# Attention and feed-forward: the second batch's visit with all remainder tiles first, its loads moved to another queue

## The chip, the cores and the metric

The kernel runs on one core of a Trainium2 chip. The metric is device time in microseconds (us) for one execution of the whole program, inputs and output in the chip's main memory (HBM). A core has five engines that run their own instruction streams and meet at semaphores: TensorE (PE, matrix products; its weight loads are listed as PEld), VectorE (DVE), ScalarE (ACT), GpSimd (POOL) and SyncE (SP). SP, ACT and POOL each issue DMA transfers; a queue issues in program order, so an issue that must wait holds up those behind it.

## The reference, cut to what matters

There are 8 batches, 12 heads, 448 tokens, 64 numbers per head. Queries and keys are normalised, scored, put through a softmax and multiplied with the values; the heads are put side by side, and two projections with a leaky ReLU between them follow.

```python
q_n = q / (norm(q, axis=-1) + 1e-06)            # q, k, v: (8, 12, 448, 64) float32
k_n = k / (norm(k, axis=-1) + 1e-06)
scores = q_n @ k_n.T / tau                      # tau = 0.1
attn = exp(scores - max) / (sum + 1e-09)
x = (attn @ v) as (8 * 448, 768)
h = x @ w_in                                    # w_in: (768, 2048)
out = maximum(0.01 * h, h) @ w_out              # w_out: (2048, 768), out: (3584, 768)
```

## The kernel before, in words

**Pairs.** Heads are taken two at a time. A pair is one batch's two neighbouring heads; there are 48, six for each batch, numbered in order, so batch 0 has pairs 0 to 5, batch 1 has 6 to 11, batch 2 has 12 to 17. Of 448 tokens, 384 are the main part (three tiles of 128) and 64 the remainder. The tile `raw_sb` has six slots for raw queries and keys; pair s uses slot s mod 6.

**What happens to a pair.** `load_qk(s)` issues four DMAs on SP (main queries, main keys, and two for the remainder rows). `load_pairs(eng, x, part, s, n)` does the same for several pairs at once, on a queue that is given. `squares(s)` squares queries and keys on GpSimd, two instructions (L182). `sums(s)` adds them up on DVE, two reduces (L193). `norm(s)` does the rest: `roots` on ACT (L200, L201: logarithm and exponential), `normalise` on DVE (L217, L218, and L222 twice, which writes the bf16 tile `qn`), and `transposes`, from pair 10 on a transposing DMA on SP (L254) into `qkT`. Then it issues loads for a later pair, and `hold`, a tiny GpSimd copy that reads `qn` and so makes GpSimd wait for it, before the squares of later pairs are queued.

**Batches and chunks.** Attention of one batch produces 448 columns of the transposed input `xT`. The projections go by chunks: chunk 0 and the other even ones have 384 tokens (three rows of 128), the odd ones 512 (four rows). In the main loop (L774 to L823) step b does three things. `visit(b)` is the second projection of chunk b (L459), and between its matmuls the scores of batch b + 1 (`key_tiles`, L280), each followed by ACT's exponential (L292). `attend_batch(b + 1)` makes the softmax sums and the products with the values of that batch (L307, L320), ACT's reciprocals (L339, L340) and DVE's scalings into `xT` (L361). `firsts(b + 1)` is the first projection of chunk b + 1 (L384), with ACT's leaky ReLU into `hT` (L391). In what follows "the second visit" is `visit(1)`: it has the second projection of chunk 1 and the scores of batch 2, that is pairs 12 to 17.

**Score tiles.** A pair has three main key tiles, each needing only its own `qkT`. The remainder keys of two pairs share one tile, so there are three remainder tiles for a batch; that of pairs 16 and 17 (written `(s0 + 5, 3)`) needs both pairs' `qkT`. From the third visit on all three stand ahead of the visit's matmuls. In the first two visits the third stands at the end (L738, L739).

**PSUM.** Eight banks are dealt by `banks`, which takes the ones given out longest ago. A visit's row of 128 tokens uses a pair of banks; at its end DVE copies both halves to SBUF (L471), in the last row of a visit ACT copies one half. The attention that follows uses the bank pairs again: `rem_products` (L307) writes sixteen products with the remainder values, eight into one pair of banks and then eight into another.

**What sets the order.** Nothing is planned by the machine: the schedule is manual, and each engine executes its instructions in the order in which the program writes them. Work for other engines is woven between PE's matmuls by tables: `norms` in the main loop names what is written after the n-th matmul step of row i of a visit, the tuples `wide`, `three`, `four` and `four_late` where a score tile is put, and `between` what is written ahead of the m-th of sixteen steps of the first projection.

**The beginning and the end.** The first pair is squared in pieces (L526 to L534), while PE runs 20 warm-up matmuls (`fill`, L505); then its `qn` is transposed by PE (L236), copied by ACT (L548) and scored. The last row of the last chunk has its second half of 384 columns computed in two parts (`second`, L410 to L429), each copied by DVE (L427) and stored in two DMAs on SP and ACT.

Of the kernel before, what the change touches and what calls it, by code (L numbers as in the profile page):

```python
# [16 lines left out]
def kernel(  # L17
# [10 lines left out]
    nc = tc.nc  # L28
# [341 lines left out]
    def chunk_cols(c):  # L370
        return (0, MAIN) if c % 2 == 0 else (MAIN, 512)
# [38 lines left out]
    def second(c, ts, half):  # L410
        last = c == B - 1 and ts == chunk_cols(c)[1] // 128 - 1
        if half == 0:
            osb[c, ts] = osp.tile([128, D_model], F32, name="osb")
        o = osb[c, ts]
        parts = 2 if last and half == 1 else 1
        for i in range(parts):
            n = HALF // parts
            lo = half * HALF + i * n
            po2 = banks(1)
            for m in range(MT):  # L420
                nc.tensor.matmul(  # L421
                    out=po2[:, :n],
                    lhsT=hT[c][:, m, ts * 128 : (ts + 1) * 128],
                    rhs=w_out_sb[:, m, lo : lo + n],
                    start=(m == 0), stop=(m == MT - 1),
                )
            nc.vector.tensor_copy(out=o[:, lo : lo + n], in_=po2[:, :n])  # L427
            if half == 1 or last:
                store(o, c, chunk_cols(c)[0] + ts * 128, lo if last else 0, lo + n, parts > 1)  # L429

    def store(o, c, x, lo, hi, apart=False):
        end, row = x + 128, 0
# [94 lines left out]
    nc.vector.tensor_tensor(sqs[0][1], k_h, k_h, op=ALU.mult)  # L527
    sums(0, (1,))
    nc.scalar.activation(sqs[0][0][:, :, 3], q_h[:, :, 3], func=AF.Square)
    for lo, hi in ((0, 3), (3, 4)):  # L530
        nc.vector.tensor_reduce(
            ss[0][:, 0:8].rearrange("p (h t) -> p h t", h=2)[:, :, lo:hi],
            sqs[0][0][:, :, lo:hi], axis=AX.X, op=ALU.add,
        )  # L534
    roots(0)
    nc.scalar.activation(sqs[1][1], k_h1, func=AF.Square)
    nc.scalar.activation(sqs[1][0], q_h1, func=AF.Square)
# [149 lines left out]

    def attend_batch(b):
        if b == 1:
            load_qk(14)  # L690
            load_qk(15)
            sums(12)
        attend_two(b * NQ)
        if b == 1:
            norm(12)
        attend(b * NQ + 2)


    def norm(s, transposed=True):
        if s >= NSLOT:  # L700
            return
        roots(s)
        normalise(s)
        if transposed:
            transposes(s)
        for x in (12, 13) if s == 11 else (s + 4,) if s > 11 else ():
            load_qk(x)
        ahead = {7: (), 8: (), 9: (10, 11), 10: (), 11: (12, 13)}.get(s, (s + 2,))
        if ahead:
            hold(qn[s][:, 6, 0, 0:1])  # L710
        for x in ahead:
            squares(x)

    def firsts(b, begun, between):

# [8 lines left out]
    def visit(b, order, norms, between):  # L724


        s0 = (b + 1) * NPAIR
        tiles = [(s0 + p, ki) for p in range(NPAIR) for ki in range(3)]
        key_tiles([(s0 + 1, 3), (s0 + 3, 3)] + [(s0 + 5, 3)] * (b > 1))
        for i, (pairs, after) in enumerate(zip(order, between)):  # L730
            last = i == len(order) - 1
            for n, _ in enumerate(groups(b, pairs, 4 if len(pairs) > 1 else 1, last), 1):
                for _ in range(after.get(n, 0)):
                    key_tiles([tiles.pop(0)])
                for fn in norms.get((i, n), ()):
                    fn()
        assert not tiles
        if b < 2:  # L738
            key_tiles([(s0 + 5, 3)])  # L739

    def at(*steps):
# [2 lines left out]
    wide = (at(8, 13, 18, 24, 29, 35, 40, 45, 50, 55, 60), at(4, 8, 12, 16, 16, 21, 26))  # L744
    three = (at(9, 16, 16, 21, 26, 31), at(5, 10, 16, 16, 21, 26, 31), at(5, 10, 16, 16, 20))
    four = (at(9, 16, 16, 24), at(4, 10, 16, 16, 24), at(4, 10, 16, 16, 24), at(5, 10, 16, 16))
    four_late = (at(5, 11, 16, 16, 24),) * 3 + (at(6, 16, 16),)

    deals["apart"] = False
    attend(NQ - 1, [lambda: first(0, 2, range(2, KT - 2)), lambda: first(0, 3, range(KT - 2))])  # L750
# [23 lines left out]
    for b in range(B):  # L774
# [6 lines left out]
        order = [[((ts, 0), (ts, 1))] for ts in range(tokens)]  # L781
        if b == 0:
            order = [order[0] + order[1], order[2]]
        norms = {(0, 18): [lambda: norm(11)]}
        if b:
            norms = {}
            for i in range(tokens - 1 + (b == 1)):
                norms[i, 4 if tokens > 3 else 12] = [lambda s=ready: norm(s)]
                ready += 1
                norms[i, 20] = [lambda s=ready: sums(s)]  # L790
        else:
            ready += 2
        visit(
            b, order, norms,
            wide if b == 0 else four_late if b == 1 else three if tokens == 3 else four,
        )
        attend_batch(b + 1)
        for j in range((b + 2) * NQ, (b + 3) * NQ):
            load_v(j)
        load_v_rem(b + 2)  # L800
        s = ready
        between = {0: [lambda s=s: norm(s)], 1: [lambda s=s: sums(s + 1)]}
        if b == 0:
            between = {
                0: [lambda: sums(13)], 1: [lambda: norm(13), lambda: sums(14)],
                4: [lambda: norm(14), lambda: sums(15)], 7: [lambda: norm(15)],
                9: [lambda: sums(16)], 11: [lambda: norm(16)], 14: [lambda: sums(17)],
            }
            ready += 5
        elif tokens == 3:  # L810
            between.update({
                4: [lambda s=s: norm(s + 1), lambda s=s: sums(s + 2)],
# [46 lines left out]
```

## Time and profile before

| what | us |
|---|---|
| median of 3 runs (406.75 to 407.87) | 406.77 |
| the profiled execution's own time | 406.75 |
| its span, first to last instruction | 404.94 |
| PE busy / ACT / DVE / POOL | 397.6 / 264.9 / 188.1 / 140.1 |
| first visit, from its first matmul of the second projection to its last score | 50.4 to 69.5 |
| attention of batch 1 | 69.9 to 76.4 |
| first projection of chunk 1 | 76.4 to 97.2 |
| second visit | 97.2 to 122.4 |

The busy time of an engine is summed over the span. A matmul's time includes its passage through the array, so matmuls that follow each other overlap in the list; their starts are what shows the pace. A line of a timeline gives start, duration, engine, source line, operation, output and input with shapes, how many instructions were merged, and in brackets the idle time before and what ended it. A line of the waits gives who waited for whom, the total, the number of times and the longest. In a table by windows, the busy time of an engine is followed by the granted clock, the share of DMA time and GB/s. "DMA to landing" is counted from the start of the issue to the last piece's arrival.

### The profile page before, as it was taken

How to read it: one execution, taken by the hardware profiler on the slowest of the kernel's cores; microseconds unless marked ns; L12 is line 12 of the kernel's file. 1: busy time of each engine (PE TensorE's matmuls, PEld its weight loads, DVE VectorE, ACT ScalarE, POOL GpSimd, SP SyncE). 2: the span in 40 equal slices, each digit the busy share in tenths (PEclk: the TensorE clock that was granted, in tenths of full speed). 3: DMA queues.
4: the chain of work that ended last, by engine and by line, in shares of the span. 5: the costliest groups of instructions: out<-in, count | busy, mean ns of one | idle time of the engine just before them, and what ended most of it. 6: DMA issues, size and time to landing. Idle time of an engine off the chain costs nothing.

```text
span 404.9 us, 10159 instructions
## 1 busy us (share of the span) xinstructions
PE 397.6 (98%) x4086; PEld 225.4 (56%) x4096; DVE 188.1 (46%) x403; ACT 264.9 (65%) x458; POOL 140.1 (35%) x213
## 2 busy tenths in 40 slices
PE   8899999999999999999999999999999999999996
PEld 3335655444555555544886555544687555544564
DVE  6987723684655624454552626256361721130021
ACT  4997799556875689655876569745786559844200
POOL 4995533464344513343142513155122500000000
PEclk9999999999999999999999999999999999999999
DMA  7999999797789827576396844685386821110033
GB/s 188 249 226 244 214 186 219 181 183 179 157 190 153 148 62 180 117 129 170 76 181 141 126 117 120 157 117 138 90 174 120 95 45 40 40 41 2 0 78 79
DMA packets 100735, 54.21 MB, mean 134 GB/s; under 512 B 69424, under 2 KB 95440, under 8 KB 100688
## 3 DMA queue, kind: packets, MB, share of 16 engines
q1 hardware_dynamic: 76400, 40.13, 42.7%
q0 software_dynamic: 23440, 12.92, 23.5%
q8 instruction: 32, 0.52, 0.6%
q10 hardware_dynamic: 848, 0.52, 0.5%
q14 instruction: 15, 0.12, 0.1%
HBM read 45.61 MB, written 11.01 MB: 140 GB/s over the span
## 4 chain that ended last, share of the span: by engine, by line
PE 96%; ACT 1%; DVE 1%; issue 0%
PE ps L384 36%; PE ps L459 31%; PE ps L320 11%; PE ps L280 8%; PE ps L421 5%; PE ps L505 2%; PE ps L307 1%; ACT pe L292 1%; PE ps L236 1%; DVE qkT L261 0%; DVE qn L222 0%; ACT qkT L548 0%; ACT rb L340 0%; DVE warm L488 0%; DVE ss L193 0%
## 5 line engine op out<-in xcount | busy, mean ns | idle before, releaser
L384 PE MATMUL ps<-xT,w_in_sb 128*128 128x384 bf16 (+1 forms) x760 | 147.4, 352 | 0.4
L459 PE MATMUL ps<-w_out_sb,hT 64*128 64x384 bf16 x1536 | 144.0, 323 | 0.0
L292 ACT ACTIVATE pe<-ps 128x896 bf16<-128x896 f32 x144 | 124.4, 917 | 16.7 <-PE ps L280 14.9
L384 PEld LDWEIGHTS <-w_in_sb 128*128 128x128 bf16 x768 | 74.1, 98 | 71.5 <-issue 3.7
L391 ACT ACTIVATE hT<-ps 128x384 bf16<-128x384 f32 (+1 forms) x128 | 67.3, 543 | 67.2 <-PE ps L384 66.7
L459 PEld LDWEIGHTS <-hT 64*128 64x128 bf16 x1536 | 84.4, 94 | 44.7 <-PE ps L459 4.2
L182 POOL TENSOR_TENSOR sq<-raw_sb 128x512 f32<-128x512 f32 x90 | 82.7, 940 | 13.4 <-DMA raw_sb<-in_k_dram 12.6
L222 DVE TENSOR_TENSOR qn<-raw_sb,r 128x512 bf16<-128x512 f32 x96 | 56.8, 634 | 1.7
L280 PE MATMUL ps<-qkT 64*128 64x448 bf16 (+1 forms) x384 | 54.8, 353 | 1.6 <-DVE qkT L261 0.8
L193 DVE TENSOR_REDUCE ss<-sq 128x6 f32<-128x384 f32 (+1 forms) x95 | 54.5, 610 | 2.6 <-POOL sq L182 2.3
L471 DVE COPY osb<-ps 128x384 f32<-128x384 f32 x41 | 21.2, 553 | 69.7 <-PE ps L459 38.8
L514 POOL CAST seen<-qn 128x1 f32<-128x1 bf16 x44 | 8.2, 187 | 123.8 <-DVE qn L222 123.6
L217 DVE TENSOR_SCALAR ss<-ss 128x14 f32<-128x14 f32 x48 | 10.0, 209 | 73.9 <-ACT ss L201 73.8
L361 DVE TENSOR_TENSOR xT<-ps,rb 128x448 bf16<-128x448 f32 x48 | 27.7, 619 | 24.3 <-ACT rb L340 24.1
L160 POOL DMA_DIRECT2D v_b<-in_v_dram x24 | 18.6, 777 | 39.9 <-PE ps L320 39.9
L320 PE MATMUL ps<-pe,v_b 128*32 128x448 bf16 x576 | 32.0, 353 | 0.0
L280 PEld LDWEIGHTS <-qkT 64*128 64x128 bf16 (+1 forms) x384 | 17.8, 97 | 17.9 <-issue 6.6
L339 ACT ACTIVATE rb<-ps 128x448 f32<-128x448 f32 x24 | 12.9, 538 | 15.3 <-PE ps L320 14.3
L320 PEld LDWEIGHTS <-v_b 128*32 128x32 bf16 x576 | 15.1, 97 | 12.0 <-issue 0.6
L427 DVE COPY osb<-ps 128x384 f32<-128x384 f32 (+1 forms) x9 | 4.6, 513 | 36.6 <-issue 22.6
L421 PE MATMUL ps<-w_out_sb,hT 128*128 128x384 bf16 (+1 forms) x144 | 21.0, 308 | 0.0
L292 ACT ACTIVATE pr<-ps 128x896 bf16<-128x896 f32 x24 | 20.7, 923 | 0.2 <-PE ps L280 0.2
(52 smaller groups left out, 188.1 us busy)
## 6 DMA issues: line engine op xcount, KB each, us to landing
raw_sb<-in_q_dram SPq DMA_DIRECT2D x46, 192.0 KB, 3.3
raw_sb<-in_k_dram SPq DMA_DIRECT2D x44, 192.0 KB, 3.5
out_dram<-osb SPq DMA_DIRECT2D x30, 192.0 KB, 3.1
v_b<-in_v_dram POOLq DMA_DIRECT2D x24, 192.0 KB, 4.8
out_dram<-osb SPq DMA_DIRECT2D x12, 384.0 KB, 2.7
w_out_sb<-in_moe_w_out_dram POOLq DMA_DIRECT2D x4, 768.0 KB, 16.3
w_in_sb<-in_moe_w_in_dram POOLq DMA_DIRECT2D x3, 512.0 KB, 8.5
w_in_sb<-in_moe_w_in_dram POOLq DMA_DIRECT2D x2, 768.0 KB, 13.1
```

The lines of the kernel that those rows point to most:

```text
L182: eng.tensor_tensor(sq, x, x, op=ALU.mult)
L193: nc.vector.tensor_reduce(o.rearrange("p (h t) -> p h t", h=2), sqs[s][i], axis=AX.X, op=ALU.add)
L222: scalings[s] = nc.vector.tensor_tensor(qn[s][:, lo:hi], x.rearrange("p h t d -> p t h d"), r[:, r0 : r0 + 2 * nt].rearrange("p (h t) -> p ...
L280: nc.tensor.matmul(out=out[:, a, :S], lhsT=x[rows, c0:c1], rhs=x[rows, 0:S], start=True, stop=True,)
L292: nc.scalar.activation(out=dst, in_=sc[:, :, :S], func=AF.Exp, scale=inv_tau)
L320: nc.tensor.matmul(out=x[32 * g : 32 * g + 32, :S], lhsT=weights(g, ki) if ki < 3 else rem(g), rhs=pe[s][:, ki, a, :] if ki < 3 else pr[j] ...
L361: scalings[j, e] = nc.vector.tensor_tensor(xT[m][:, 2 * jj + e, half * S : (half + 1) * S], pos.pop((j, e))[:, :S], rbs[j], op=ALU.mult,)
L384: nc.tensor.matmul(out=pm[:, :n], lhsT=w_in_sb[:, kt, m * 128 : (m + 1) * 128], rhs=xT[c // 2][:, kt, c0 : c0 + n], start=(kt == 0), stop= ...
L391: nc.scalar.activation(out=hT[c][:, m, :n], in_=pms.pop((c, m))[:, :n], func=AF.Prelu, alpha=0.01)
L421: nc.tensor.matmul(out=po2[:, :n], lhsT=hT[c][:, m, ts * 128 : (ts + 1) * 128], rhs=w_out_sb[:, m, lo : lo + n], start=(m == 0), stop=(m = ...
L459: done[p][i] = nc.tensor.matmul(out=pos2[p][:, i, :HALF], lhsT=hT[c][rows, m, ts * 128 : (ts + 1) * 128], rhs=w_out_sb[rows, m, half * HAL ...
L471: copy(out=osb[c, ts][:, half * HALF : (half + 1) * HALF], in_=po2[:, i, :HALF])
```

## The change

Four things are changed.

- At the beginning, the squares of the first pair's keys go from DVE to ACT, between ACT's squares of its main and of its remainder queries; DVE sums them behind the first reduce of the queries.
- The last half row's two parts are 256 and 128 columns wide instead of 192 and 192.
- The second visit has all three remainder tiles at its beginning and uses the table `four` of the later visits; `four_late` goes. So pairs 12 to 17 are all normalised before it: `sums(12)` is written after step 26 of the first visit's last row, `norm(12)` ahead of the attention of batch 1 and `sums(13)` in its middle, and pairs 13 to 17 follow in the first projection of chunk 1. The second visit normalises three pairs instead of four.
- Pairs 14 and 15 are no longer loaded by SP at the beginning of `attend_batch(1)` but by four DMAs on GpSimd's queue, behind the squares of pair 12 and ahead of those of pair 13; pairs 16 and 17 by four more behind the squares of pair 14. SP's loads of pairs 19, 20 and 21 all follow the normalising of pair 17. The values of batch 2 are loaded (on GpSimd's queue, seven DMAs) at step 8 of the first projection, behind the squares of pair 18, instead of ahead of it.

```diff
     def second(c, ts, half):
-        parts = 2 if last and half == 1 else 1
-        for i in range(parts):
-            n = HALF // parts
-            lo = half * HALF + i * n
+        widths = (HALF * 2 // 3, HALF // 3) if last and half == 1 else (HALF,)
+        for i, n in enumerate(widths):
+            lo = half * HALF + sum(widths[:i])
...
     nc.scalar.activation(sqs[0][0][:, :, 0:3], q_h[:, :, 0:3], func=AF.Square)
-    nc.vector.tensor_tensor(sqs[0][1], k_h, k_h, op=ALU.mult)
-    sums(0, (1,))
+    nc.scalar.activation(sqs[0][1], k_h, func=AF.Square)
     nc.scalar.activation(sqs[0][0][:, :, 3], q_h[:, :, 3], func=AF.Square)
     for lo, hi in ((0, 3), (3, 4)):
         nc.vector.tensor_reduce(
...
+        if lo == 0:
+            sums(0, (1,))
...
     def attend_batch(b):
         if b == 1:
-            load_qk(14)
-            load_qk(15)
-            sums(12)
+            norm(12)
         attend_two(b * NQ)
         if b == 1:
-            norm(12)
+            sums(13)
         attend(b * NQ + 2)
...
     def norm(s, transposed=True):
-        for x in (12, 13) if s == 11 else (s + 4,) if s > 11 else ():
+        for x in {11: (12, 13), 14: (18,), 17: (19, 20, 21)}.get(s, (s + 4,) if s > 17 else ()):
             load_qk(x)
...
-        for x in ahead:
+        for i, x in enumerate(ahead):
             squares(x)
+            if s in (11, 12) and i == 0:
+                for part in range(2):
+                    for y in (q, k):
+                        load_pairs(gp, y, part, 14 + 2 * (s - 11), 2)
...
     def visit(b, order, norms, between):
-        key_tiles([(s0 + 1, 3), (s0 + 3, 3)] + [(s0 + 5, 3)] * (b > 1))
+        key_tiles([(s0 + 1, 3), (s0 + 3, 3)] + [(s0 + 5, 3)] * (b > 0))
...
-        if b < 2:
+        if b == 0:
             key_tiles([(s0 + 5, 3)])
...
-    four_late = (at(5, 11, 16, 16, 24),) * 3 + (at(6, 16, 16),)
...
-        norms = {(0, 18): [lambda: norm(11)]}
+        norms = {(0, 18): [lambda: norm(11)], (1, 26): [lambda: sums(12)]}
         if b:
-            for i in range(tokens - 1 + (b == 1)):
+            for i in range(tokens - 1):
...
         attend_batch(b + 1)
-        for j in range((b + 2) * NQ, (b + 3) * NQ):
-            load_v(j)
-        load_v_rem(b + 2)
+        def values(b=b + 2):
+            for j in range(b * NQ, (b + 1) * NQ):
+                load_v(j)
+            load_v_rem(b)
+        if b:
+            values()
...
             between = {
-                0: [lambda: sums(13)], 1: [lambda: norm(13), lambda: sums(14)],
-                4: [lambda: norm(14), lambda: sums(15)], 7: [lambda: norm(15)],
-                9: [lambda: sums(16)], 11: [lambda: norm(16)], 14: [lambda: sums(17)],
+                0: [lambda: norm(13)], 1: [lambda: sums(14)],
+                2: [lambda: norm(14)], 3: [lambda: sums(15)],
+                4: [lambda: norm(15)], 5: [lambda: sums(16)],
+                7: [lambda: norm(16)], 8: [lambda: sums(17), values],
+                9: [lambda: norm(17)], 13: [lambda: sums(18)],
             }
-            ready += 5
+            ready += 6
```

More of the change, by code (lines that the diff above doesn't have):

```diff
@@ L428, in second @@
             if half == 1 or last:
-                store(o, c, chunk_cols(c)[0] + ts * 128, lo if last else 0, lo + n, parts > 1)
+                store(o, c, chunk_cols(c)[0] + ts * 128, lo if last else 0, lo + n, len(widths) > 1)
     def store(o, c, x, lo, hi, apart=False):
@@ L792 @@
             ready += 2
[L793 to L796, printed above, removed]
+        visit(b, order, norms, wide if b == 0 else three if tokens == 3 else four)
         attend_batch(b + 1)
-        for j in range((b + 2) * NQ, (b + 3) * NQ):
-            load_v(j)
-        load_v_rem(b + 2)
+        def values(b=b + 2):
[4 more added lines that the diff above has]
+            values()
         s = ready
```

## The prediction, made before the result was known

> **What bounds the kernel now.** I read the page's busy times first, then TensorE's waits, then the timelines of the stages that the change touches.
>
> ```profile
> PE 397.6 (98%) x4086; PEld 225.4 (56%) x4096; DVE 188.1 (46%) x403; ACT 264.9 (65%) x458; POOL 140.1 (35%) x213
> ```
>
> ```profile
> PE ps L505 <- DVE warm L488: 1.5, 1, 1.5
> PE ps L280 <- DVE qkT L261: 0.8, 2, 0.5
> PE ps L280 <- ACT pe L292: 0.5, 2, 0.3
> PE ps L280 <- ACT qkT L548: 0.2, 1, 0.2
> PE ps L236 <- DVE qn L222: 0.2, 1, 0.2
> ```
>
> PE is busy for 98% of the span, and its waits are 3.2 us in all, every one of them before 24 us. From there to 401 us matmuls stand end to end, so anything that keeps PE waiting there is paid in full at the end, and what the other engines save there is worth nothing. Gains can only come from the opening, from fewer switches in PE's own order, and from the last store.
>
> The sum is made against the profiled execution: 406.75 us, of which 404.94 is the span and 1.81 lies around it; the median of the three runs is 406.77, so the two may be exchanged. About 0.3% (1.22 us) is what a measurement of this kernel can tell from no change.
>
> **Part 1, the opening: the first keys' squares go from DVE to ACT.**
>
> ```profile
> 4.37 0.56 DVE L527 TENSOR_TENSOR sq<-raw_sb 128x384 f32<-128x384 f32 x1 [1.66 <-DMA raw_sb<-in_k_dram]
> 4.96 0.55 DVE L193 TENSOR_REDUCE ss<-sq 128x6 f32<-128x384 f32 x1
> 5.43 0.74 DVE L531 TENSOR_REDUCE ss<-sq 128x6 f32<-128x384 f32 x2
> ...
> 8.06 0.59 PE L505 MATMUL ps<-warm 128*128 128x512 bf16 x2
> ...
> 8.49 0.28 PE L236 MATMUL ps<-id,qn 128*128 128x128 bf16 x2
> ```
>
> On ACT the square costs 0.52 us (its twin, L526), and fits between that one's end at 4.53 and the wait for the remainder rows, which ends at 5.40. DVE loses 0.56 us. The last reduce then waits only for ACT's remainder square (5.40 + 0.31 = 5.71) and ends near 6.02 instead of 6.17: pair 0's keys are normalised 0.15 us earlier. But the first transposes start at 8.49 behind the warm-up matmuls, with nothing waited for: their queries were ready near 7.97, their keys at 8.44, and the keys' turn comes only at 8.72. Everything after hangs on ACT's copy of those transposes. So I take 0.00; the warm-up is the cover. Ends: -1.7 us, all the waits listed above after the first, and +0.3, if the remainder square comes late by most of the keys' square.
>
> **Part 2, the end of the first visit: sums of pair 12 in front of a PSUM copy.** DVE now does pair 12's two reduces before the last copy of the visit; it did them after.
>
> ```profile
> 67.76 1.82 POOL L182 TENSOR_TENSOR sq<-raw_sb 128x512 f32<-128x512 f32 x2 [10.26 <-DMA raw_sb<-in_k_dram]
> 69.71 0.56 DVE L471 COPY osb<-ps 128x384 f32<-128x384 f32 x1 [5.47 <-PE ps L459]
> 70.05 0.65 PE L307 MATMUL ps<-pr,v_rem 64*32 64x448 bf16 x16
> 70.19 1.14 DVE L193 TENSOR_REDUCE ss<-sq 128x8 f32<-128x512 f32 x2
> ```
>
> GpSimd's squares of pair 12 run from 67.76 (they waited for the load, whose issue is not moved) to 69.58. The second reduce can start at 69.61; two reduces in a row stand 0.47 us apart from what follows, so the copy starts near 70.08 instead of 69.71. PE's sixteen remainder products use two bank pairs; the second pair is the one that this copy and ACT's copy empty. In the trace its second matmul starts at 70.32, 0.05 after the copy's end, so the copy is already what PE waits for. It moves to 70.64 + 0.05 = 70.69: **+0.37 us** on PE, where nothing else can run. Behind that copy wait also the third store (unhurried) and the matmuls after. Ends: 0 (the load lands 0.37 earlier) and +1.1 (both reduces, if it lands a few tenths later).
>
> Pair 12's normalisation before the attention hides: ACT's two root operations (0.31 + 0.21) fit between its exponential, which ends at 71.02, and the logarithm that starts at 71.43 and is itself pushed to 71.80. DVE's four (0.17 + 0.24 + 1.16 and gaps, 1.6 us) end near 73.1, where the scalings, pushed by 0.37 too, begin: 0.06 late, without a reader in haste.
>
> **Part 3, loads and squares during the second first-projection.** PE reaches the second visit at 97.25 + 0.37 = 97.62, and its third remainder tile, with pair 17, near 98.05. Before, that tile stood at 122.06. So pair 17's transposing DMA must have landed by 98.05. The chain:
>
> - GpSimd's four load issues cost 0.81 + 0.76 + 0.64 + 0.63 = 2.84 us (the same four at 28.88 to 31.67). The first four run 69.5 to 72.4 and push the squares of pair 13 from 69.5 to 72.4, where they cost nothing: DVE reads them at 75.2. Pairs 14 and 15 then land, by the 3.5 us of a lone GpSimd load and some 1.7 us for each 384 KB more at 230 GB/s, near 76.5; squares of 14 to 78.3; the next four issues to 81.2; squares of 15 to 83.2; pairs 16 and 17 land near 85; squares of 16 to 86.9, of 17 to 88.7.
> - DVE and ACT go in turn: normalise a pair (1.6 us), sum the next (1.1), roots (0.6), 3.3 us in all. From scalings that end at 77.7: pair 13 at 79.3, 14 at 83.2 (it waits for ACT's second hT), 15 at 86.6, 16 at 89.9, 17 at 93.2. GpSimd is ahead at each step, by 0.2 to 0.5 us for pairs 15 and 16. The transposing DMA of 17 is issued at 93.3. On SP it is behind those of 15 and 16 and the load of 18, all issued by 91.5; the loads of 19 to 21 now follow it.
>
> ```profile
> 187.76 1.26 SPq L254 DMA_TRANSPOSE qkT<-qn  x1
> ...
> DMA to landing us min/median/max: 3.0/5.5/6.9
> ```
>
> The first line is its like in the fourth batch, issued 3.93 us ahead of the visit at 191.69 and landed after 2.9. The second gives the four landings between 80 and 98 us. The high ones, 6.5 to 6.9, are those beside the second batch's value loads. The change moves these value loads to GpSimd's queue behind the squares of pair 18, that is to 92 to 97 us, just beside pair 17. Landing: 96.2 with 2.9, 97.8 with 4.5 (the middle of the ends 2.9 and 6.9, since SP's own loads no longer stand ahead), 100.2 with 6.9. I take 97.8: in time, **0.00**, ends 0 and +2.2 us.
>
> By the Trainium skill, DMA: Bandwidth & Descriptors, Queues, rings and completion order, each DMA engine goes round-robin between the queues that have work, packet by packet. By that rule the transpose shares the engines with the values and its own transfer would at most about double, which the 6.9 of the trace exceeds.
>
> ACT's hT passes wait up to 1.8 us for the roots of pair 17, hidden by eight banks of 1.3 us each. Value loads are needed by 123: hidden. Pair 19's load, now behind pair 17's transpose on SP, is squared by 102; the next PSUM copies behind its sums on DVE are due at 104.8: hidden, 2 us to spare.
>
> The moved loads are now issued by GpSimd. By the Trainium skill, SBUF — State Buffer, SBUF: two separate sides, a GpSimd-issued DMA can starve while DVE holds the port they share, 620 ns becoming some 3100. The four issues at 28.88 to 31.67 took 0.63 to 0.81 us with DVE busy beside them, so the trace does not bear it out.
>
> **Part 4, PE's order in the second visit.** It becomes that of the later four-row visits.
>
> ```profile
> 97.25:122.37 25.12, 25.12 (x305) 1.00 0.74 168
> 191.69:216.74 25.05, 25.05 (x307) 1.00 0.67 144
> ```
>
> From the first score to the attention's first product the second visit takes 25.12 us, its twin in the fourth batch 25.05 (and the one in the sixth): **-0.07**. The remainder products after it take 0.71 us to the next group (122.37 to 123.08) against 0.69 (216.74 to 217.43), since one wait on a DVE copy goes: **-0.02**. Ends 0 and -0.3.
>
> **Part 5, the last part is 256 + 128 columns instead of 192 + 192.** Start to start a matmul took 162.5 ns for 384 columns and 82.5 for 192; that line gives 109 and 56 (transposes of 128 columns: 56). 16 x (109 + 56) is 2.64 us, as is 32 x 82.5. The final copy shrinks by 64 columns:
>
> ```profile
> 398.74 0.56 DVE L427 COPY osb<-ps 128x384 f32<-128x384 f32 x1 [2.03 <-PE ps L421]
> ...
> 401.32 0.36 DVE L427 COPY osb<-ps 128x192 f32<-128x192 f32 x1 [0.89 <-PE ps L421]
> ```
>
> 0.201 us less for 192 columns less, so **-0.07**. The part before is stored 0.43 later but its issue on both queues (0.57) is over by 401.55, before the last copy ends at 401.6. Ends -0.2 and +0.3.
>
> **Sum.** 0.00 + 0.37 + 0.00 - 0.09 - 0.07 = +0.21; 406.75 + 0.21 = 406.96, say 407.0.
>
> **Rivals.**
> - Pair 17 lands late (slower). Place: third remainder tile of the second visit, PE waiting. From 98.05 each us is paid; it passes the 0.3% bound when the landing is later than 99.06, which is a latency over 5.7 or a chain 1.2 us behind. For: 6.9 and 6.5 stand in the trace beside value loads, and GpSimd's lead is thin. Against: those had loads ahead in SP's queue. At 6.9: 406.96 + 2.2 = 409.2. Chance 0.19.
> - The copy is not delayed (the load of pair 12 lands earlier, or DVE has done both reduces): 406.96 - 0.37 = 406.6. Against: GpSimd's start at 67.76 is the load's landing. Chance 0.12.
> - GpSimd's eight load issues take longer beside DVE's work: a tenth more for each uses up the lead of 0.2 to 0.5 us, and 2 us beyond give 409. Against: the longest issue on GpSimd's row is 0.85 us. Chance 0.04. (It is what the page on SBUF would have.)
> - The opening does hang on the first keys' squares (faster): all 1.7 us of PE's waits go, 406.96 - 1.7 = 405.3; it decides from 1.4 on. Against: the warm-up in front. Chance 0.05.
>
> **Numbers.** The forecast has 0.60. Faster by over 0.3%: 0.05; slower: 0.19 + 0.04 = 0.23; within: 0.72. Low end 406.4: the second rival less 0.2 from the open ends. High end 408.7: about half of the slower cases. Left out: 0.05 below, some 0.12 above.
>
> **What would show it.** First transposes at 8.49 as before; the L471 copy near 70.1 and the second bank's remainder products near 70.7; the second visit 25.05 long; its third remainder tile with no wait on a DMA; a last copy of 0.29 us. Wrong if PE shows a wait of more than 1 us near 98, or if hT passes hold it between 80 and 97.

## The result, and the profile after

The changed kernel takes 416.66 us, the median of six runs (415.73 to 418.61), where the kernel before takes 406.83 beside it. The ratio is 1.024, 95% interval 1.022 to 1.027: it is slower by 2.4%, and the forecast of 407.0 and its range were wrong. The profiled execution of the changed kernel took 418.61 us with a span of 416.8. It is 2 us above the median of its runs, so the terms below add up to 11.9 us, the difference of the two profiled spans, and not to 9.8. Many lines of the code have moved up by one: L459 is now L458, L471 is L470, L427 is L426, L505 is L504.

The page's busy times and the granted clock, the lines of it that answer to the first fence of the prediction:

```profile
PE 402.2 (96%) x4096; PEld 226.4 (54%) x4096; DVE 192.6 (46%) x402; ACT 265.1 (64%) x459; POOL 146.9 (35%) x221
...
PEclk9999999999599999999999999999999999999999
```

PE has nearly the same list of matmuls and is busy 4.6 us longer, and in one slice its clock was granted at half. TensorE's waits in the changed kernel:

```profile
PE ps L280 <- DMA qkT<-qn: 6.7, 1, 6.7
PE ps L504 <- DVE warm L487: 1.5, 1, 1.5
PE ps L307 <- DVE osb L470: 1.1, 1, 1.1
PE ps L280 <- DVE qkT L261: 0.6, 2, 0.3
...
PE ps L458 <- DMA w_out_sb<-in_moe_w_out_dram: 0.2, 1, 0.2
```

Before, the list had the warm-up and tenths of a microsecond at the start. Two new lines stand out: 6.7 us for a transposing DMA at the scores, and 1.1 us for DVE's PSUM copy at the remainder products. TensorE by stages (stretch, length, busy time and matmuls, clock, DMA share, GB/s), the first projection of chunk 1, the second visit, and a part of that visit:

```profile
78.47:99.30 20.83, 20.83 (x101) 1.00 0.51 117
99.30:134.43 35.13, 28.34 (x305) 0.85 0.90 164
107.50:112.70 5.20, 5.20 (x36) 0.50 0.78 195
```

The first projection is as long as before (76.42 to 97.25 was 20.83 too). The second visit took 25.12 and now takes 35.13: 6.79 us idle, and 3.22 us more busy time for the same matmuls. The last line says why: at a clock of 0.50 each matmul takes twice as long. By finer stretches the clock fell at about 102.6, in the middle of the wait, and rose again at about 112.8. From the end of the wait at 107.04 on that is 5.8 us of work at half clock, and half of it, 2.9, is the loss. The account of the 11.9 us:

| where | us | read from |
|---|---|---|
| start of the first visit, 50.43 to 50.72 | +0.29 | differs from run to run (50.28 to 50.79 in the profiles below that keep `hold`) |
| rest of the first visit | +0.42 | 0.2 of it is the wait for a load of `w_out` |
| the copy ahead of the remainder products | +1.34 | the sixteen remainder products with the values at L307, 1.92 instead of 0.58 |
| first projection of chunk 1 | 0.00 | 20.83 in both |
| second visit, idle | +6.79 | 35.13 - 28.34 |
| second visit, longer matmuls | +3.22 | 28.34 - 25.12, of which 2.9 by the clock |
| all that follows | -0.16 | the remainder |

The copy first. The timeline of the changed kernel at the end of the first visit:

```profile
69.45 1.82 POOL L182 TENSOR_TENSOR sq<-raw_sb 128x512 f32<-128x512 f32 x2 [11.67 <-DMA raw_sb<-in_k_dram]
70.52 1.34 DVE L193 TENSOR_REDUCE ss<-sq 128x8 f32<-128x512 f32 x2 [5.58 <-POOL sq L182]
71.77 0.55 DVE L470 COPY osb<-ps 128x384 f32<-128x384 f32 x1
72.37 0.38 PE L307 MATMUL ps<-pr,v_rem 64*32 64x448 bf16 x7 [1.07 <-DVE osb L470]
```

The mechanism is as forecast: DVE waits 5.58 us for the squares, the PSUM copy stands behind the two reduces, PE behind the copy. But the load of pair 12 landed at 69.45 where I had taken 67.76 as fixed, and PE itself was 0.7 later.

Now pair 17. Instructions on the tile `qkT` between 98 and 108 us, with who waited and the time from issue to landing; then TensorE's timeline after the wait:

```profile
L254 SPq DMA_TRANSPOSE qkT<-qn x1: 1242/1242/1242, 99.2 to 99.2; - x1
...
  PE ps L280: 6.7, 1
...
DMA to landing us min/median/max: 7.8/7.8/7.8
```

```profile
107.04 0.58 PE L280 MATMUL ps<-qkT 64*64 64x448 bf16 x2 [6.72 <-DMA qkT<-qn]
107.55 3.06 PE L458 MATMUL ps<-w_out_sb,hT 64*128 64x384 bf16 x18
```

The transposing DMA is issued at 99.19 and lands at 106.99. PE begins the second visit at 99.30 and stands before the third remainder tile from 100.32 on. Two things made it late. The issue stands 20.7 us after the first projection's beginning (78.47) where the prediction had 16.5 (93.3 less 76.79). And the landing took 7.8 us where it had 4.5. Why the issue is late is in the timelines of GpSimd and DVE, and in DVE's waits between 78 and 100 us:

```profile
79.34 0.17 DVE L217 TENSOR_SCALAR ss<-ss 128x14 f32<-128x14 f32 x1
79.78 2.27 POOL L182 TENSOR_TENSOR sq<-raw_sb 128x512 f32<-128x512 f32 x2 [3.41 <-DMA raw_sb<-in_k_dram]
79.81 2.66 DVE L222 TENSOR_TENSOR qn<-raw_sb,r 128x512 bf16<-128x512 f32 x2
82.00 0.81 POOL L127 DMA_DIRECT2D raw_sb<-in_q_dram  x1
...
84.14 0.66 DVE L217 TENSOR_SCALAR ss<-ss 128x14 f32<-128x14 f32 x1 [0.62 <-ACT ss L201]
84.93 2.30 POOL L182 TENSOR_TENSOR sq<-raw_sb 128x512 f32<-128x512 f32 x2
85.11 2.53 DVE L222 TENSOR_TENSOR qn<-raw_sb,r 128x512 bf16<-128x512 f32 x2
...
89.03 1.04 POOL L182 TENSOR_TENSOR sq<-raw_sb 128x512 f32<-128x512 f32 x1 [1.14 <-DMA raw_sb<-in_k_dram]
...
97.14 0.52 DVE L217 TENSOR_SCALAR ss<-ss 128x14 f32<-128x14 f32 x1 [0.62 <-ACT ss L201]
97.57 2.31 POOL L160 DMA_DIRECT2D v_b<-in_v_dram  x3
```

```profile
DVE ss L217 <- ACT ss L201: 2.5, 4, 0.6
DVE xT L361 <- ACT rb L340: 0.2, 1, 0.2
```

GpSimd waits 3.41 us for pair 14, whose load, issued from 71.2 on, came at 79.7 instead of 76.5; 1.7 of these 3.2 us are the later start, since pair 12 had landed late. Only behind the squares of pair 14 can the loads of pairs 16 and 17 be issued (82.0), and they land at 88.9 instead of 85.

Yet DVE did not wait for any of these squares: its waits in this stretch are for ACT alone. What the late data did was to move GpSimd's squares and load issues beside DVE's normalising, and there DVE's rows grow. The two multiplies (L222) take 1.16 us together when no square runs beside them; here they took 2.66 for pair 13, beside the squares at 79.78, and 2.53 for pair 14, beside those at 84.93. The small L217, 0.17 alone, took 0.45 to 0.79 in pairs 14 to 17. Over the five pairs these rows took 11.54 us where alone they would take 6.65, 4.9 us more. With the scalings before them, which end at 79.4 instead of 77.7, that is why pair 17's normalising begins at 97.14 instead of 91.6 (93.2 less 1.6). The last line of the timelines is the values, issued from 97.57 on, right beside the transposing DMA.

The end answers to Part 5. DVE's last copies in the changed kernel:

```profile
412.54 0.42 DVE L426 COPY osb<-ps 128x256 f32<-128x256 f32 x1 [1.20 <-PE ps L420]
413.37 0.29 DVE L426 COPY osb<-ps 128x128 f32<-128x128 f32 x1 [0.40 <-PE ps L420]
```

### The profile page after: what moved, and what is told of

It reads as the page before. It is cut to its first block, busy times and chain, and to the rows that moved or that the text cites. A ratio compares the mean times of both kernels' runs of the same rounds, so it can differ in the third digit from the quotient of the medians.

```text
span 416.8 us, 10146 instructions
## 1 busy us (share of the span) xinstructions
PE 402.2 (96%) x4096; PEld 226.4 (54%) x4096; DVE 192.6 (46%) x402; ACT 265.1 (64%) x459; POOL 146.9 (35%) x221
## 4 chain that ended last, share of the span: by engine, by line
PE 81%; DMA 13%; POOL 3%; ACT 2%; issue 1%; DVE 1%; POOLq 0%
PE ps L384 31%; PE ps L458 28%; PE ps L320 10%; PE ps L280 6%; PE ps L420 5%; DMA w_out_sb<-in_moe_w_out_dram 4%; DMA w_in_sb<-in_moe_w_in_dram 4%; DMA qkT<-qn 2%; DMA raw_sb<-in_q_dram 2%; POOL sq L182 1%; ACT pe L292 1%; PE ps L307 1%; DMA raw_sb<-in_k_dram 1%; POOL raw_sb L132 0%; POOL v_rem L167 0%
## 5 line engine op out<-in xcount | busy, mean ns | idle before, releaser
L458 PE MATMUL ps<-w_out_sb,hT 64*128 64x384 bf16 x1536 | 146.7, 327 | 0.2 <-DMA w_out_sb<-in_moe_w_out_dram 0.2
L458 PEld LDWEIGHTS <-hT 64*128 64x128 bf16 x1536 | 85.3, 95 | 46.4 <-issue 5.4
L391 ACT ACTIVATE hT<-ps 128x384 bf16<-128x384 f32 (+1 forms) x128 | 66.4, 544 | 62.2 <-PE ps L384 61.9
L182 POOL TENSOR_TENSOR sq<-raw_sb 128x512 f32<-128x512 f32 x90 | 83.8, 951 | 23.8 <-DMA raw_sb<-in_k_dram 23.2
L280 PE MATMUL ps<-qkT 64*128 64x448 bf16 (+1 forms) x384 | 55.7, 355 | 8.2 <-DMA qkT<-qn 6.7
L222 DVE TENSOR_TENSOR qn<-raw_sb,r 128x512 bf16<-128x512 f32 x96 | 60.7, 673 | 2.0 <-DMA raw_sb<-in_k_dram 0.3
L470 DVE COPY osb<-ps 128x384 f32<-128x384 f32 x41 | 21.2, 553 | 66.5 <-PE ps L458 30.7
L217 DVE TENSOR_SCALAR ss<-ss 128x14 f32<-128x14 f32 x48 | 10.8, 225 | 79.8 <-ACT ss L201 79.8
L320 PEld LDWEIGHTS <-v_b 128*32 128x32 bf16 x576 | 15.2, 97 | 11.9 <-issue 0.6
L426 DVE COPY osb<-ps 128x384 f32<-128x384 f32 (+2 forms) x9 | 4.6, 514 | 36.5 <-issue 23.0
L420 PE MATMUL ps<-w_out_sb,hT 128*128 128x384 bf16 (+2 forms) x144 | 21.0, 308 | 0.0
```

The costliest lines, as they stand in the source:

```text
L182: eng.tensor_tensor(sq, x, x, op=ALU.mult)
L222: scalings[s] = nc.vector.tensor_tensor(qn[s][:, lo:hi], x.rearrange("p h t d -> p t h d"), r[:, r0 : r0 + 2 * nt].rearrange("p (h t) -> p ...
L280: nc.tensor.matmul(out=out[:, a, :S], lhsT=x[rows, c0:c1], rhs=x[rows, 0:S], start=True, stop=True,)
L320: nc.tensor.matmul(out=x[32 * g : 32 * g + 32, :S], lhsT=weights(g, ki) if ki < 3 else rem(g), rhs=pe[s][:, ki, a, :] if ki < 3 else pr[j] ...
L391: nc.scalar.activation(out=hT[c][:, m, :n], in_=pms.pop((c, m))[:, :n], func=AF.Prelu, alpha=0.01)
L420: nc.tensor.matmul(out=po2[:, :n], lhsT=hT[c][:, m, ts * 128 : (ts + 1) * 128], rhs=w_out_sb[:, m, lo : lo + n], start=(m == 0), stop=(m = ...
```

## The experiments

Theory: the wait of 6.7 us for pair 17 and the copy are the whole loss, and the wait has three causes that add up, the loads on GpSimd's queue, the values beside the transposing DMA, and half clock after the wait. Rivals: the order in the second visit itself costs; the changes at the two ends cost; the sums ahead of the copy cost most.

**The two ends alone.** To the kernel before, one of the two changes each.

```diff
-    nc.vector.tensor_tensor(sqs[0][1], k_h, k_h, op=ALU.mult)
-    sums(0, (1,))
+    nc.scalar.activation(sqs[0][1], k_h, func=AF.Square)
...
+        if lo == 0:
+            sums(0, (1,))
```

> The kernel before with the first keys' squares on ACT alone. Theory (the opening hides behind the warm-up matmuls): first transposes at 8.49 us as before, time 406.8, within 0.2 of before. Rival (the opening is part of the loss: TensorE reached the first visit 0.29 us later in the changed kernel): 407.1, with ACT's remainder square or the copy after it later than before.

```diff
-        parts = 2 if last and half == 1 else 1
+        widths = (HALF * 2 // 3, HALF // 3) if last and half == 1 else (HALF,)
...
```

> The kernel before with parts of 256 and 128 columns at the end alone. Theory: the last copy takes 0.29 instead of 0.36 us, time 406.7 (0.07 less). Rival (the second store now waits for the first one's issue on both queues): 407.0 to 407.2.

The first took 407.05 (11 runs) beside 406.86, ratio 1.0004 (0.9995 to 1.0013). Its first transposes began at 8.11 and not at 8.49 as expected, but by 13.2 us PE was where it had been before. The second took 406.80 (11 runs), ratio 0.9996 (0.9988 to 1.0005). Neither can be told from no change. The last copy in the second, DVE's timeline:

```profile
401.69 0.29 DVE L426 COPY osb<-ps 128x128 f32<-128x128 f32 x1 [0.40 <-PE ps L420]
```

The 0.07 us is there in the row; in the time it is below what eleven runs resolve.

**The sums of pair 12 back behind the copy.** The changed kernel with one line moved; the loads and the values stay.

```diff
+            sums(12)
             norm(12)
...
-        norms = {(0, 18): [lambda: norm(11)], (1, 26): [lambda: sums(12)]}
+        norms = {(0, 18): [lambda: norm(11)]}
```

> The changed kernel with the sums of pair 12 written after the first visit again, so behind the PSUM copy on DVE. Theory (the losses add up: about 1.3 us at the copy, the rest at pair 17): the wait of TensorE for that copy goes, pair 12 is normalised no later, time 1.3 less than the changed kernel's 416.7, that is 415.4. Rival (what comes later absorbs it, since TensorE then arrives 1.3 us earlier at a third remainder tile whose pair 17 is no earlier): the wait at the third tile grows by 1.3 and the time stays 416.7.

It took 415.64 (4 runs), ratio 1.020 (1.018 to 1.022), 1.0 us below the changed kernel. The wait at L307 is gone from TensorE's waits, and the large one stays:

```profile
PE ps L280 <- DMA qkT<-qn: 6.2, 2, 5.8
PE ps L504 <- DVE warm L487: 1.5, 1, 1.5
```

So the copy is a small part of the loss; the rival that it costs most falls.

**The third remainder tile back at the end of the second visit.** All loads and squares stay where the change put them.

```diff
-        key_tiles([(s0 + 1, 3), (s0 + 3, 3)] + [(s0 + 5, 3)] * (b > 0))
+        key_tiles([(s0 + 1, 3), (s0 + 3, 3)] + [(s0 + 5, 3)] * (b > 1))
...
-        if b == 0:
+        if b < 2:
             key_tiles([(s0 + 5, 3)])
```

> The changed kernel with the second visit's third remainder tile at its end again, everything else as changed. Theory (pair 17 is late, by 6.7 us in the changed kernel's profile, and the clock drop that follows the wait costs 2.6 more): both go, no slow clock, time 407.5 to 408.5; only the 1.3 us at the copy and some tenths stay. Rival (the loads on GpSimd's queue cost TensorE elsewhere as well): waits come up at other score tiles or at hT, time over 410.

It took 412.28 (4 runs), ratio 1.013 (1.012 to 1.015). I had expected 407.5 to 408.5. The wait for pair 17 is gone, but another came up. TensorE's waits, and DVE's between 100 and 112 us:

```profile
PE ps L280 <- DVE osb L470: 3.2, 1, 3.2
```

```profile
DVE ss L193 <- POOL sq L182: 6.1, 1, 6.1
```

DVE waits 6.1 us for the squares of pair 19, whose load landed at 107.7; the PSUM copies of the visit stand behind the sums, and PE behind the copies. In the changed kernel this second wait does not show, since the larger one had already held PE up: there DVE had the sums done by 113.3 and waited for PE until its next copy at 116.30.

**The values later.** The values of batch 2 written at step 14 of the first projection, behind the squares of pair 19.

```diff
-                7: [lambda: norm(16)], 8: [lambda: sums(17), values],
-                9: [lambda: norm(17)], 13: [lambda: sums(18)],
+                7: [lambda: norm(16)], 8: [lambda: sums(17)],
+                9: [lambda: norm(17)], 13: [lambda: sums(18)], 14: [values],
```

> The changed kernel with the value loads of batch 2 written six steps later, behind the squares of pair 19, so that they no longer run beside pair 17's transposing DMA. Theory (both the chain and the value loads make pair 17 late): its DMA lands about 3 us after its issue instead of 7.8, the wait at the third tile shrinks from 6.7 to about 2, and the clock falls less or not at all: 409 to 412. Rival (the value loads do not matter, the DMA is slow for another reason): landing after 6 us or more, time 416 to 417.

It took 410.23 (4 runs), ratio 1.009 (1.007 to 1.011), 6.4 us below the changed kernel. Instructions on the tile `qkT` between 96 and 101 us:

```profile
  PE ps L280: 2.0, 1
...
DMA to landing us min/median/max: 2.9/2.9/2.9
```

Issued 20.7 us after the first projection's beginning, as late as in the changed kernel, the transposing DMA lands in 2.9 us instead of 7.8. The 4.9 us between are the value loads beside it. The wait that is left, 2.0 us, was not followed by half clock (mean clock 1.00). The profiled execution is the fastest of the four, 409.33; two of the others, 410.70 and 411.35, had mean clocks of 0.995 and 0.994, and their waits are not on record.

**The loads of pairs 14 to 17 on SP, pair by pair.** The values stay where the change put them.

```diff
+            load_qk(14)
+            load_qk(15)
             norm(12)
...
-        for x in {11: (12, 13), 14: (18,), 17: (19, 20, 21)}.get(...):
+        for x in {11: (12, 13), 12: (16,), 13: (17,), 14: (18,), 17: (19, 20, 21)}.get(...):
...
-            if s in (11, 12) and i == 0:
-                for part in range(2):
-                    for y in (q, k):
-                        load_pairs(gp, y, part, 14 + 2 * (s - 11), 2)
```

> The changed kernel with pairs 14 to 17 loaded by SP, pair by pair, as before. Rival (GpSimd's load issues and their late landing are what makes pair 17 late): its transposing DMA is issued by 94 instead of 99.2 us and lands in time, 408 to 409. Theory (the chain of DVE and ACT and the value loads make it late whatever the queue): issue 1 to 3 us earlier at most, the wait at the third tile still 3 us or more, 412 to 416.

It took 412.02 (4 runs), ratio 1.012 (1.010 to 1.014), 4.6 us below the changed kernel. TensorE's waits, and TensorE by stretches around the end of the wait:

```profile
PE ps L280 <- DMA qkT<-qn: 3.1, 1, 3.1
...
PE ps L307 <- DVE osb L470: 0.8, 1, 0.8
```

```profile
102.00:103.00 1.00, 0.67 (x4) 0.58 1.26 231
103.00:104.00 1.00, 1.00 (x8) 0.50 1.58 202
104.00:105.00 1.00, 1.00 (x8) 0.50 1.39 291
105.00:106.00 1.00, 1.00 (x12) 0.72 1.05 250
```

The transposing DMA of pair 17 is issued 18.5 us after the first projection's beginning instead of 20.7, so GpSimd's queue cost 2.2 us, and lands after 6.2 us beside the values. The 2.2 us are those of DVE's rows: L217 and L222 of pairs 13 to 17 take 2.6 us longer than alone here, and 4.9 in the changed kernel. Half clock also follows a wait of 3.1 us.

**PE kept busy in the wait.** The changed kernel with 30 warm-up matmuls ahead of the third remainder tile, whose results nobody uses: this kernel does work that the reference has not.

```diff
+            if (s, ki) == (17, 3):
+                fill(30)
```

> The changed kernel with 30 idle matmuls of 512 columns (6.5 us, results unused) ahead of the second visit's third remainder tile. Theory (the half clock after the wait comes from TensorE having stood still): pair 17 lands as before, TensorE does not fall to the half clock, and the 2.6 us of slow matmuls behind it go: 414 to 415. Rival (the clock falls for another reason, or the fall costs nothing): 416.7 or, with the fill behind the wait, more.

It took 413.50 (4 runs), ratio 1.016 (1.014 to 1.017), 3.2 us *below* the changed kernel, with 30 matmuls more. TensorE from the second visit's first score on:

```profile
97.00:129.10 32.10, 32.10 (x338) 1.00 0.93 180
```

No idle time and a clock of 1.00 throughout, where the changed kernel had 0.85. The transposing DMA still took 6.9 us to land. So half clock follows from PE's idling, not from what PE does afterwards. Not all of the 3.2 us is the clock's: in the profile of this kernel the wait for the PSUM copy was missing too, which may be why the time is below the 414 to 415 expected.

**The sums ahead, alone.** To the kernel before, pair 12's two reduces ahead of the copy, nothing else.

```diff
-            sums(12)
...
-        norms = {(0, 18): [lambda: norm(11)]}
+        norms = {(0, 18): [lambda: norm(11)], (1, 26): [lambda: sums(12)]}
```

> The kernel before with one step of the change alone: pair 12's two reduces on DVE ahead of the first visit's last PSUM copy. Theory (the copy waits for GpSimd's squares of pair 12, and so for its load; TensorE waits for the copy): TensorE's second remainder products start late by as much as those squares start after about 67.4 us, 0.4 in a run like that of before; time 407.0 to 407.5, with single runs up to 1.3 over 406.9. Rival (TensorE makes it up later): 406.9.

It took 406.99 (11 runs), ratio 1.0004 (0.9993 to 1.0014); single runs reached 408.0 and 408.2. In its profile the squares of pair 12 begin at 67.44, and the first projection behind the attention of batch 1 begins 0.05 us later than in the kernel before (76.47 against 76.42). The time cannot be told from no change. The two longest runs fit the theory without proving it, since they have no profile.

**Without `hold`.** The kernel before without the small GpSimd copies that keep later squares behind a pair's normalising.

```diff
-        if ahead:
-            hold(qn[s][:, 6, 0, 0:1])
```

> The kernel before without the small GpSimd copies (hold) that keep the squares of later pairs behind a pair's normalisation, so that GpSimd's squares run whenever their load has landed, beside DVE's normalisation too. Theory (a square on GpSimd and a normalising multiplication on DVE slow each other, as the changed kernel's rows of 1.2 to 1.6 us instead of 0.55 and 0.69 suggest): more such long rows than the four or so of before, where the two overlap and nowhere else; time 407 to 409. Rival (those rows are long for another reason, such as the load issues beside them): durations as before, 0.69 and 0.55, time 406.5 to 407.

It took 410.30 (4 runs), ratio 1.008 (1.006 to 1.010), slower than the 407 to 409 expected. DVE's groups of lines by form (total busy us, mean ns, idle before), in this kernel and in the kernel before:

```profile
L222 DVE TENSOR_TENSOR qn<-raw_sb,r 128x512 bf16<-128x512 f32 x48 | 37.5, 781 | 1.7
...
L222 DVE TENSOR_TENSOR qn<-raw_sb,r 128x384 bf16<-128x384 f32 x48 | 31.5, 656 | 0.0
...
L217 DVE TENSOR_SCALAR ss<-ss 128x14 f32<-128x14 f32 x48 | 26.0, 541 | 56.9 <-ACT ss L201 56.8
```

```profile
L222 DVE TENSOR_TENSOR qn<-raw_sb,r 128x512 bf16<-128x512 f32 x48 | 33.5, 698 | 1.7
...
L222 DVE TENSOR_TENSOR qn<-raw_sb,r 128x384 bf16<-128x384 f32 x48 | 27.3, 569 | 0.0
...
L217 DVE TENSOR_SCALAR ss<-ss 128x14 f32<-128x14 f32 x48 | 10.0, 209 | 73.9 <-ACT ss L201 73.8
```

The same instructions take longer when GpSimd's squares are free to run beside them: the small one 541 ns instead of 209, the two multiplies 83 and 87 ns more on the mean. Of 17 rows of L222 over 0.8 us 16 overlap a square, and the other one overlaps load issues of GpSimd.

**Two and three of the moves undone together.** From the edits above: the third tile at the end with the values late; the loads on SP with the values late; and the latter with the sums behind the copy too, which leaves of the change the order in the second visit, the earlier normalising and the two ends.

> The changed kernel with the third remainder tile at the end of the second visit and the value loads behind pair 19's squares. With the tile at the end alone TensorE waited 3.2 us for a PSUM copy that stood on DVE behind the sums of pair 19. Theory (the value loads also make pair 19 late, since its load comes behind pair 17's transpose and beside them): that wait goes or falls under 1 us, time 407 to 409. Rival (pair 19 is late because its load is issued late, whatever runs beside it): the wait stays at 2 to 3 us, 411 to 412.

> The changed kernel with two of the three steps undone: pairs 14 to 17 loaded by SP and the values behind pair 19's squares; pair 12's sums stay ahead of the copy. Theory (either step alone left 412.0 and 410.2, both are needed to have pair 17 in time, and the copy's wait is worth 0 to 1.3 us a run by when pair 12's load lands): no wait at the third tile, time 406.8 to 407.6 and more spread than the 406.35 to 407.26 with all three undone. Rival (the sums ahead of the copy also make the normalising late, so that pair 17 misses its tile): a wait for its DMA of 1 us or more, 408 to 409.

> The changed kernel with three steps undone together: pair 12's sums behind the copy, pairs 14 to 17 loaded by SP, the values behind pair 19's squares. What stays of the change is the early normalising, all three remainder tiles at the front of the second visit, the opening and the last part. Theory (these three steps carry the loss): pair 17's transposing DMA is issued 18.5 us after the first projection begins, lands about 3 us later, just when it is due; TensorE waits there 0.5 us at most, the clock stays, time 406.6 to 407.5. Rival (the early normalising of six pairs doesn't fit in whatever the loads do): a wait of 1 us or more at the third tile or the copies after it, 408 to 411.

| kernel | median us | ratio to before | 95% |
|---|---|---|---|
| third at the end, values late (10 runs) | 406.88 | 1.0002 | 0.9992 to 1.0013 |
| loads on SP, values late (11 runs) | 407.26 | 1.0014 | 1.0005 to 1.0023 |
| loads on SP, values late, sums behind (11 runs) | 406.70 | 0.9995 | 0.9986 to 1.0004 |

The times of the second and the third lie in their expected ranges, that of the first just below its own. In the first the wait of 3.2 us is gone: pair 19 is squared at 102.3 instead of 107.7. The second's waits of TensorE show what is left, in a profiled execution of 408.39, the high end of its runs:

```profile
PE ps L307 <- DVE osb L470: 1.1, 1, 1.1
...
PE ps L280 <- DMA qkT<-qn: 0.4, 1, 0.4
```

In the third no wait is left, the transposing DMA of pair 17 lands in 2.9 us at 97.36, and the second visit is, in TensorE by stages:

```profile
97.19:122.24 25.05, 25.05 (x307) 1.00 1.15 201
```

From its first score to the attention's first product the visit takes 25.05 us, where it took 25.12 before. So the order of the second visit costs nothing by itself, that rival falls; the 0.07 us that it saves is far below what the times resolve. With the three moves undone the whole loss is gone. No version clearly beats the kernel before.

The moves do not add up one by one. Undone alone, the sums give 1.0 us, the loads 4.6 and the values 6.4, 12.0 in all where the loss is 9.8, since the loads and the values shorten the same wait. The third tile alone gives 4.4, since the next late thing then takes its place. Each of these differences also holds some tenths for the copy, whose wait goes with the landing of pair 12 and was missing in some profiles.

## Why the prediction was wrong

**Part 3 failed, at "I take 97.8: in time, 0.00, ends 0 and +2.2 us".** Pair 17's own time was wrong at each of its two steps, and what stood behind it was not in the sum.

- *The chain to the issue, 93.3.* It came 4.2 us late relative to the first projection. The step that failed is "normalise a pair (1.6 us)". The chain began on time: pair 13's normalising stood 0.9 us behind the first projection's beginning, as forecast (77.7 against 76.79). After that DVE waited for no square, only for ACT's roots, 0.6 us a pair, which the 3.3 us had in it. But its own rows were 4.9 us longer than alone, because GpSimd's squares and load issues ran beside them; 0.6 of that went into the wait for ACT's hT that I had allowed at pair 14. I had asked only whether GpSimd would be ahead of DVE. What its work does to DVE's rows while it runs beside them I had put at nothing, without a reason.
- *The late loads behind it.* They decide how much of GpSimd's work meets the normalising. In the six kernels with these loads on GpSimd's queue the rows are 2.8 to 4.9 us longer than alone, in the three with the loads on SP 1.2 to 2.6. Even with all three moves undone the 3.3 us is too short: DVE's cycle is 3.56 to 3.65 us, of which 0.42 to 0.51 is L217, 0.17 in the rows that I had read. The chain then begins 2.0 us behind the projection's beginning, and the issue stands 18.1 us behind it, where I had 16.5. The rival "issues take longer" did not happen (0.63 to 0.82 us each).
- *The landing, 4.5.* The middle of 2.9 and 6.9 is 4.9 and not 4.5, and with it pair 17 would have landed at 98.2, already behind the 98.05 at which it was due. The middle was the wrong choice besides, and the upper end was no bound: 7.8, 7.4, 6.9, 6.8 and 6.2 in five kernels with the values beside it, 2.9 in four without. In these four the next pair's transposing DMA has the values beside it instead, and it takes 6.5 to 8.6. So the values are the cause, and the argument that the high ones of before came from SP's own queue is not borne out. By the Trainium skill, DMA: Bandwidth & Descriptors, Queues, rings and completion order, each DMA engine goes round the queues packet by packet; my estimate from it, a transfer at most about doubled, takes the packets of both queues as equally long, and 2.9 to 7.8 is more than that.
- *What a late landing costs.* I priced it at 1 us for each us. The wait of 6.7 brought half clock on top, 2.9 us. This term was in no rival, and the rival "pair 17 lands late" gave 409.2 as its time.
- *Pair 19's load, "hidden, 2 us to spare".* It is not: 3.2 us of wait once pair 17's is out of the way, with the values late none. It was hidden in the changed kernel only by the larger wait.

**Part 2: mechanism right, size by the landing.** In place of +0.37 the trace has +1.34. The delay goes with the time at which pair 12's load lands, for which I had taken one execution's 67.76. Squares beginning at 67.44 go with no wait of PE (sums ahead, alone), at 68.59 with a wait of 0.8 us (loads on SP), at 69.45 with one of 1.1 us. The upper end of +1.1 came closer, but it was argued from the two reduces; the wait for the squares ahead of them is what counts.

**Parts 1, 4 and 5 right.** At the beginning DVE's last reduce ended at 5.93 (forecast 6.02), the first transposes began at 8.53, behind the warm-up. With the wait out of the way the second visit took the forecast 25.05 us, and the remainder products behind it 0.69 (122.24 to 122.93). The last copy is 0.29 us long. That hT passes would not hold PE held too, since the first projection kept its 20.83 us. Terms of 0.1 us are seen in rows only; no time here resolves them.

**The range.** The rivals went one at a time. DVE's longer rows, the values and the clock all meet at one tile, and the high end of 408.7 was laid halfway into a rival that had only one of them.

## What to carry to other kernels

A move that brings a deadline forward by 24 us has to be laid out against every transfer that now falls beside it, not against the rows of the old place: here the values made a 2.9 us transfer one of 6.2 to 7.8. It is not enough that the engine that feeds another is done in time: ask also what it runs beside, since here the feeding engine slowed the fed one by 4.9 us without ever letting it wait. A landing time is a row of one execution; where an engine that waits for it stands ahead of something that TensorE needs, take the spread of landings and not the one seen. And if TensorE would idle for 3 us or more, price the wait with the half clock that follows, and ask what the next late thing behind it is.

## What the runs showed of the hardware

**Half clock after a wait.** The granted TensorE clock fell to 0.50 with waits of 6.7 us (changed kernel), 3.2 (third tile at the end) and 3.1 us (loads on SP), and not with the 2.0 us in the profile with the values late. It fell 2.2 us into the first of these waits and 3.0 us into the last, and in the 3.2 us case 0.5 us after the wait was over. It stayed at half for 10.2 us with the longest wait, 6.8 with one of 5.8 us (sums behind) and 3.4 each with the other two: three times, twice and once the same length. Only what is left of such a stretch when work resumes is paid, 5.8 of the 10.2 us. By the Trainium skill, TensorE: Matmul & The Clock Gate, Part 1, an idle window of about 3.4 us lets the clock fall to half and a busy one brings it back; the length of the stretches and the 2.0 us agree, but a wait did not have to last 3.4 us: those of 3.1 and 3.2 us were enough, and in the longest the clock fell after 2.2.

**DVE's normalising and GpSimd's squares hardly run at once.** Where no square overlaps it, the 128x512 multiply of L222 takes 691 to 694 ns in the kernel before (46 of 48) and in the changed one (43 of 48); all rows of L222 over 800 ns in both kernels, ten in number, overlap a square. At 79.8 in the changed kernel two multiplies and two squares together take from 79.78 to 82.47, 2.69 us; alone they take 1.16 and 1.82, which is 2.98 in a row. By the Trainium skill, SBUF — State Buffer, SBUF: two separate sides, VectorE and GpSimd hold a pair of ports in turn for the whole instruction, and a VectorE operation with two SBUF inputs is one that takes it against a GpSimd operation reading SBUF; 2.69 of 2.98 agrees with nearly that. I had drawn on the same section for starving DMA issues, which did not occur, and passed over this part of it.

The small L217, with one tensor input, does not run slowly but waits. In the fourteen traces of this case 92 of its 672 rows are longer than 0.25 us (0.17 alone), and every one of them ends within 0.11 us of the end of a square or a load issue on GpSimd. In the changed kernel it ends at 97.66 where the square ended at 97.63, and at 84.80 where the fourth load issue ended. Without `hold` its longest row took 3.94 us, while issues and squares of GpSimd followed one another. What holds it was not tried.
